# Gate and value products of a convolution and SwiGLU kernel: from f32 products in a 15-product form to three float32r passes in an 11-product form

## The chip, the cores and the metric

The kernel runs on one core of a Trainium2 chip. Its engines are TensorE (PE, with its weight loads shown apart as PEld), VectorE (DVE), ScalarE (ACT), GpSimd (POOL) and SyncE (SP), which issues most DMA transfers. Work is kept in SBUF, matmuls write to PSUM. The metric is the device time of one execution in microseconds (us); the kernel before takes 2593.32 us, the median of three runs (2593.27 to 2593.45).

## The reference

Eight sequences of 4096 tokens of width 192 pass a causal convolution of seven taps, the same taps for the 24 channels of a head, and the result passes a gated feed-forward block without bias:

```python
w = np.exp(weight - max); w = w / (sum(w) + 1e-09)          # 8 heads x 7 taps
out[b, s, h] = sum_k w[h, k] * x_pad[b, s + k, h]           # x: (8, 4096, 192)
x = out.reshape(32768, 192)
xn = x / sqrt(mean(x * x) + 1e-06) * rms_g
g = xn @ w_gate;  val = xn @ w_val                          # (192, 1536) each
return (g / (1 + exp(-g)) * val) @ w_out                    # (1536, 192)
```

All arrays are f32 or are read as f32.

## The kernel before, in words

**Tiling.** Tokens are taken in 32 *pairs* of 2 x 512. Width 192 is three slices of 64 rows. Gate weights lie on partitions 0 to 63 and value weights on 64 to 127, and so does x, twice; so each product is two half instructions (64 rows by 128 columns of weights, 512 tokens), one for the gate and one for the value, on the two halves of the array at once. The 1536 hidden channels are 12 blocks of 128.

**Products.** Pair 0 is computed plainly (`plain`, L1052, and `outer`, L1093) while the weights, which come as 64-bit floats, are being converted. From pair 1 on, four *units* of three channel blocks each need 18 products (three slices, two token groups, three blocks); the table `CHAINS` of the class `Unit` reaches them with 15 products (L794) on sums of weights (`WSUM`, made once on POOL, L365/L369) and sums of x (`XSUM`, L705, on DVE and POOL for each pair). Products run into each other in PSUM: copies of a bank (L743 on ACT, L747 on DVE) fork a chain, sums (L810, L814, L820, L826) join it, silu (L839) and a product (L846) make the hidden activations `ht`.

**Output.** A seven-product form of the output matmul takes sums of `ht` (L962, POOL) and 42 *steps*, each of six column-tiled matmuls (L934); its results are joined (L983), transposed (L949) and stored (L1016).

**What a pair prepares for later pairs.** `load_heads` brings x (L146); the taps (`part_tap`, L468 on ACT, then L476 on DVE) accumulate in PSUM; squares (L492), a reduction (L503), a power (L512) and a scaling (L530) give the normalized x, which is stored to a scratch tensor in DRAM (L670) and fetched back, transposed, as `xb` (L696).

**Order.** The order is written out by hand and by tables: `ORDER` is one string of words, run once for each pair. `p2` emits two steps of TensorE; other words name an engine (A, V, G, D) and an action. Every engine runs its instructions in the order in which they were emitted, and waits on semaphores for others.

The printed functions below are those that the change touches.

Of the kernel before, what the change touches and what calls it, by code (L numbers as in the profile page):

```python
# [11 lines left out]
F32 = mybir.dt.float32  # L12
AF = mybir.ActivationFunctionType
ALU = mybir.AluOpType
# [5 lines left out]
def kernel(  # L20
# [45 lines left out]
    XOP = (5, 6, 9, 0, 15, 14, 4, 7, 13, 10, 2, 11, 12, 8, 3)  # L66
    XSUM = (
        (0, 1, 4), (1, 2, 6), (2, 0, 6), (9, 3, 5), (3, 3, 8), (4, 7, 15), (5, 4, 15), (6, 5, 7),
        (7, 0, 1), (8, 1, 2), (9, 8, 15),
    )  # L70
    WSUM = (
        (9, "sub", 5, 2), (9, "sub", 9, 8), (10, "sub", 1, 4), (10, "add", 7, 10),
        (11, "sub", 1, 8), (7, "sub", 7, 11), (11, "sub", 4, 11), (12, "add", 1, 6),
        (4, "sub", 12, 4), (5, "sub", 5, 4), (5, "add", 3, 5), (13, "sub", 2, 6),
        (13, "add", 0, 13), (14, "sub", 3, 12), (3, "sub", 6, 3), (0, "add", 0, 3),
        (3, "sub", 3, 2), (6, "neg", 6, 6), (8, "neg", 8, 8),
    )
    WAT = (7, 9, 2, 0, 1, 4, 5, 11, 14, 6, 10, 12, 8, 3, 13)

    SPAN = 1509
    ORDER = (  # L90
        "p2 GX4- VT11- p2 AS40.0.0 GX9- AS40.1.0 p2 AF0.1.0 AF0.0.0 p2 VC.0.0 Dload- p2",
        "VC.1.0 AS41.0.0 VS41.1.0 p2 AS00.1.0 VS00.0.0 p2 Vbc- VD5.0.0 Gmul- p2 VD5.1.0",
        "AS42.0.0 VS42.1.0 AS51.1.0 p2 AS51.0.0 VR1.0.0 p2 VR1.1.0 VR0.0.0 p2 AF2.0.0 VN.1.0",
        "AG0.0.0 p2 VR0.1.0 AF3.0.0 Dplace- AF3.1.0 p2 GM0.1.0 VR2.0.0 p2 VR2.1.0 AS44.1.0",
        "AS44.0.0 VR5.1.0 p2 AG2.0.0 VR3.0.0 p2 GM2.1.0 AS40.0.1 VR3.1.0 AS40.1.1 p2 VR5.0.0",
        "AG4.0.0 p2 VM4.1.0 AF0.0.1 AG5.0.0 VF0.1.1 p2 AG1.0.0 VS41.0.1 GM5.1.0 p1 AS41.1.1",
        "p1 VC.0.1 AG3.0.0 p1 VC.1.1 p1 GM3.1.0 VS00.0.1 p2 AS42.0.1 VS42.1.1 AS00.1.1 GS3.0",
        "p2 VD5.0.1 p1 VD5.1.1 p1 AS51.0.1 GS1.0 VR1.0.1 AS51.1.1 p2 VR1.1.1 AF2.0.1 GS3.1 p2",
        "AF2.1.1 VR0.0.1 AG1.0.1 p1 VR0.1.1 p1 GM1.1.1 VF3.0.1 AF3.1.1 p2 AG0.0.1 VR2.0.1 p1",
        "VR2.1.1 p1 GM0.1.1 AS44.0.1 AS44.1.1 VR5.0.1 p2 GS2.0 VR5.1.1 p2 AS40.0.2 VR3.1.1",  # L100
        "AS40.1.2 p1 VR3.0.1 GM1.1.0 p1 AG4.0.1 AG3.0.1 p1 VM4.1.1 p1 GM3.1.1 VF0.0.2 AF0.1.2",
        "p2 AS41.0.2 VS41.1.2 p1 AG5.0.1 p1 VC.0.2 GM5.1.1 p1 VC.1.2 p1 AS00.0.2 AS00.1.2 p2",
        "GS1.1 AS42.1.2 AS42.0.2 p2 VD5.0.2 GS3.2 p1 VD5.1.2 p1 AS51.0.2 VR1.0.2 AS51.1.2 p2",
        "GS2.1 VR1.1.2 AF2.0.2 p2 AF2.1.2 VR0.0.2 GS1.2 AG1.0.2 p1 VR0.1.2 p1 AG0.0.2 VF3.0.2",
        "GM1.1.2 p1 AF3.1.2 p1 VR2.0.2 AG2.0.1 p1 VR2.1.2 p1 AS44.0.2 GM2.1.1 AS44.1.2 p2",
        "VR3.0.2 AG2.0.2 GS2.2 p1 VR3.1.2 p1 AS40.0.3 VR5.0.2 AS40.1.3 p2 GM2.1.2 AG4.0.2",
        "VR5.1.2 AG3.0.2 p1 VM4.1.2 p1 AF0.0.3 GM0.1.2 p2 AF0.1.3 VS41.0.3 AS41.1.3 p2",
        "GM3.1.2 AG5.0.2 VC.0.3 p1 VC.1.3 p1 AS00.1.3 GS3.3 AS00.0.3 p2 VS42.0.3 AS42.1.3 p2",
        "GS1.3 VD5.0.3 p1 VD5.1.3 p1 AS51.0.3 GM5.1.2 VR1.0.3 AS51.1.3 p2 VR1.1.3 AF2.0.3 p2",
        "GS2.3 AF2.1.3 VR0.0.3 AG1.0.3 p1 VR0.1.3 p1 GS4.2 VF3.0.3 AF3.1.3 p2 AS44.0.3",  # L110
        "VS44.1.3 p1 GM1.1.3 p1 VR5.1.3 p1 VR5.0.3 p1 Acv0_1 VR3.0.3 AG5.0.3 p1 Vcv1_1 Acv0_2",
        "GM5.1.3 p2 VR3.1.3 AG0.0.3 p2 AG3.0.3 Vcv1_2 DfetA GS3.4 p1 AG4.0.3 p1 VR2.0.3 p2",
        "Acv0_0 Vcv2_2 GM3.1.3 p2 VM4.1.3 p2 Vcv2_1 Ac1 GS3.5 p1 AG2.0.3 p1 Vcv3_1 p2 GS1.4",
        "Vcv3_2 p2 Vcv1_0 p2 GS2.4 p1 Vcv2_0 p2 Vcv4_1 p1 As7 GS1.5 DfetB Dst0- p1 VR2.1.3 p2",
        "Vcv5_1 p1 GM0.1.3 p1 Vcv3_0 p2 Vcv6_1 p1 GS2.5 p1 Vcv4_0 p2 Vcv4_2 GS4.0 p2 Vcv5_0",
        "p2 GS4.1 p1 Vcv6_0 p2 Vcv5_2 Ac2 p1 GX0 p1 Vcv6_2 p2 VM2.1.3 Asq p2 GS4.4 p4 VX3 p1",
        "GS4.3 p4 VX6 p1 GX2 p2 VC22 p2 VX1 p2 GS4.5 VT22 p2 Vred p2 GX8 p3 GX7 p2 VC21 p2",
        "VT21 Gpow p2 VX5 p2 VX10 p2 VT12 p1 Dst1 p1",
# [16 lines left out]
    def load_heads(p, b, t0):  # L135
# [4 lines left out]

        def get(dst, tb, h, dims, r):
            row = x[b, t0 + tb * TB + r - HALO, h * GS :]
            src = bass.AP(
                tensor=row.tensor, offset=row.offset, ap=[dims, [D, TB + HALO - r], [1, GS]]
            )
            nc.sync.dma_start(out=dst, in_=src)  # L146

        first = 0
        if t0 == 0:
            nc.gpsimd.memset(t[0:H, 0:HALO, :], 0.0)  # L150
            get(t[0:H, HALO:, :], 0, 0, [GS, H], HALO)
            first = 1
        for h in range(H):
            get(t[first * H + h :: H], first, h, [TB * D, P // H - first], 0)
# [206 lines left out]
    def w_sums(u):  # L361
        t = wf[u]
        for i, (d, op, a, b) in enumerate(WSUM):
# [9 lines left out]
            if i % 4 == 3:  # L373
                yield
# [935 lines left out]
```

## Time and profile before

| what | value |
|---|---|
| median of 3 runs | 2593.32 us |
| span of the profiled execution | 2591.8 us |
| TensorE busy, granted clock | 2580.5 us, 1.00 |
| DVE, POOL, ACT busy | 2298.8, 2190.6, 1553.5 us |
| first product of pair 1 | at 126.37 us |
| products of one pair, then output steps | 51.92 us, 27.44 us |
| a stretch 1000 to 1052 us (products): DVE, ACT, POOL busy | 45.75, 42.31, 41.37 us |
| a stretch 1052 to 1079.4 us (output): DVE, ACT, POOL busy | 25.76, 5.78, 27.09 us |
| DMA | 137.33 MB, 53 GB/s on the mean |

The profile is one execution. In a group's row stand the line, the engine and operation, the tiles out and in with their shapes, the count, the busy time and mean duration of one, and the idle time ahead of it with its releaser. Matmuls are pipelined, so the mean of one is longer than the distance between two. The chain of work that ended last names at each step what released it; shares of it, not of busy time, tell what sets the end.

### The profile page before, as it was taken

Reading aid. Unit: us, or ns where it says so; the run is one execution under the profiler, and the core shown is the slowest. Engines: PE = TensorE matmul, PEld = TensorE weight load, DVE = VectorE, ACT = ScalarE, POOL = GpSimd, SP = SyncE. Lnnn points to the kernel's source line nnn. Section 1 sums busy time; section 2 is a strip of 40 time slices with the busy share of each in tenths; the row PEclk is TensorE's granted clock in tenths of the full one; section 3 lists DMA queues with packets and bytes.
Section 4 is the critical chain, followed back from the end, with each engine's and each line's share of the span. In section 5 each row is a group of like instructions: output and inputs, shape, how many; then the busy total and the mean of one; then the engine's idle time right before and its main releaser. Section 6 shows DMA issues by size and latency. Waiting matters only on the chain.

```text
span 2591.8 us, 60798 instructions
## 1 busy us (share of the span) xinstructions
PE 2580.5 (100%) x23872; PEld 1778.0 (69%) x23872; DVE 2298.8 (89%) x3681; ACT 1553.5 (60%) x2825; POOL 2190.6 (85%) x1791
## 2 busy tenths in 40 slices
PE   9999999999999999999999999999999999999999
PEld 6876666767667666676666676666766666766667
DVE  8898898988989989989889899899898898988975
ACT  6576555675555765556755557655566555676554
POOL 4898888988889888898888898888988888988877
PEclk9999999999999999999999999999999999999999
DMA  6232332222331323322223313233222233122210
GB/s 145 57 57 33 63 64 52 44 45 51 63 63 38 57 33 64 63 49 47 45 51 64 62 38 55 36 63 63 46 49 45 52 63 58 37 56 40 50 44 14
DMA packets 512397, 137.33 MB, mean 53 GB/s; under 512 B 483950, under 2 KB 486510, under 8 KB 512110
## 3 DMA queue, kind: packets, MB, share of 16 engines
q1 hardware_dynamic: 508364, 132.53, 27.2%
q8 instruction: 187, 3.06, 0.5%
q10 hardware_dynamic: 3746, 0.92, 0.2%
q14 instruction: 100, 0.82, 0.1%
HBM read 83.84 MB, written 49.55 MB: 51 GB/s over the span
## 4 chain that ended last, share of the span: by engine, by line
PE 99%; DVE 0%; issue 0%; DVEq 0%
PE ps L794 62%; PE ps L934 33%; PE ps L1052 2%; PE ps L1093 1%; DVE xb L647 0%; DVE wf L338 0%; DVE xc L333 0%; DVE o_sb L949 0%; DVE xc L298 0%; DVE xc L303 0%; DVE xc L306 0%; DVEq L1305 0%
## 5 line engine op out<-in xcount | busy, mean ns | idle before, releaser
L794 PE MATMUL ps<-xc,wf 64*128 64x512 f32 x4960 | 1214.0, 591 | 0.0
L794 PEld LDWEIGHTS ps<-xc,wf 64*128 64x128 f32 x4960 | 681.3, 186 | 375.3 <-issue 176.7
L794 PE MATMUL ps<-xb,wf 64*128 64x512 f32 x2480 | 679.7, 591 | 0.0
L743 ACT ACTIVATE tile<-ps 128x512 f32<-128x512 f32 x678 | 391.1, 593 | 389.0 <-PE ps L794 295.3
L743 ACT ACTIVATE tls<-ps 128x512 f32<-128x512 f32 (+1 forms) x562 | 323.5, 589 | 438.6 <-PE ps L794 222.0
L846 POOL TENSOR_TENSOR ht<-ht,tile 128x512 f32<-128x512 f32 x329 | 418.9, 1275 | 141.0 <-ACT tile L839 65.2
L794 PEld LDWEIGHTS ps<-xb,wf 64*128 64x128 f32 x2480 | 353.9, 187 | 182.9 <-issue 93.6
L846 POOL TENSOR_TENSOR ht<-ht,tls 128x512 f32<-128x512 f32 x260 | 330.6, 1274 | 86.4 <-ACT tls L839 38.8
L743 ACT ACTIVATE ps<-ps 128x512 f32<-128x512 f32 (+1 forms) x589 | 336.0, 580 | 87.9 <-PE ps L934 32.6
L962 POOL TENSOR_TENSOR early<-ht 128x512 f32<-128x512 f32 x279 | 354.8, 1276 | 4.9
L476 DVE SCALAR_TENSOR_TENSOR ps<-xh,tp,ps 128x512 f32<-128x512 f32 x450 | 320.3, 748 | 4.0 <-ACT ps L468 1.8
L934 PE MATMUL ps<-ht,wo_sb 128*32 128x128 f32 (+2 forms) x5208 | 318.5, 380 | 0.0
L934 PEld LDWEIGHTS ps<-ht,wo_sb 128*32 128x32 f32 x5208 | 233.9, 110 | 81.7 <-POOL ht L846 23.5
L934 PE MATMUL ps<-ht,x 128*32 128x128 f32 (+2 forms) x4464 | 250.7, 379 | 0.0
L826 DVE TENSOR_TENSOR tile<-ps,tile 128x512 f32<-128x512 f32 x349 | 237.4, 683 | 10.2 <-PE ps L794 5.0
L962 POOL TENSOR_TENSOR ht<-ht 128x512 f32<-128x512 f32 x186 | 239.0, 1285 | 4.9
L826 DVE TENSOR_TENSOR ht<-ps,tile 128x512 f32<-128x512 f32 x328 | 222.5, 680 | 6.5 <-ACT tile L743 6.5
L934 PEld LDWEIGHTS ps<-ht,x 128*32 128x32 f32 x4464 | 184.3, 110 | 61.3
L839 ACT ACTIVATE tile<-tile 128x512 f32<-128x512 f32 x349 | 214.5, 625 | 0.0
L826 DVE TENSOR_TENSOR ht<-ps,tls 128x512 f32<-128x512 f32 x292 | 199.0, 681 | 6.8 <-ACT tls L743 3.6
L826 DVE TENSOR_TENSOR tls<-ps,tls 128x512 f32<-128x512 f32 x271 | 184.9, 683 | 17.0 <-PE ps L794 13.8
L934 PE MATMUL ps<-early,x 128*32 128x256 f32 (+2 forms) x3348 | 196.0, 379 | 0.0
(149 smaller groups left out, 3278.1 us busy)
## 6 DMA issues: line engine op xcount, KB each, us to landing
xb<-xd SPq DMA_DIRECT2D x120, 384.0 KB
xd<-yn SPq DMA_DIRECT2D x244, 96.0 KB
xh<-in_x_dram SPq DMA_DIRECT2D x192, 105.0 KB
out_dram<-o_sb SPq DMA_DIRECT2D x122, 96.0 KB
out_dram<-o_sb SPq DMA_DIRECT2D x60, 128.0 KB
xh<-in_x_dram SPq DMA_DIRECT2D x56, 98.4 KB
out_dram<-o_sb SPq DMA_DIRECT2D x122, 32.0 KB
ht<-in_moe_w_gate_dram SPq DMA_DIRECT2D x12, 192.0 KB
```

The source lines that it names most:

```text
L476: nc.vector.scalar_tensor_tensor(out=dst, in0=xk, scalar=w, in1=at, op0=ALU.mult, op1=ALU.add)
L743: nc.scalar.activation(out=dst, in_=src, func=AF.Copy, scale=float(s))
L794: nc.tensor.matmul(out=self.new(v, h, True) if first else self.old(v, h), lhsT=wf[self.u][HALF[h], WAT[i], :], rhs=x_op(XOP[i])[HALF[h]], ...
L826: nc.vector.tensor_tensor(out=self.hv(v) if h else t[:], in0=self.old(v, h), in1=t[:], op=plus(s))
L839: nc.scalar.activation(out=t[:], in_=src[:], func=AF.Silu)
L846: engine[eng].tensor_tensor(out=self.hv(v), in0=src, in1=t[:], op=ALU.mult)
L934: nc.tensor.matmul(out=self.bank(b)[i * Q : (i + 1) * Q, at : at + n], lhsT=left, rhs=cols, start=fresh, stop=True, skip_group_check=True, ...
L962: engine[eng].tensor_tensor(out=dst, in0=a, in1=b, op=op)
L1052: nc.tensor.matmul(out=bank(h, bks[h])[:], lhsT=wf[u][HALF[h], AT[h][k] * NF + f, :], rhs=xb[HALF[h], g, k, :], start=(k == 0), stop=(k == ...
L1093: nc.tensor.matmul(out=bank(h, bks[h])[:, w : w + D], lhsT=hts[f // NF][HALF[h], g, f % NF, j * P : (j + 1) * P], rhs=wo_sb[HALF[h], f, :] ...
```

## The change

The gate and value products of pairs 2 to 31 are done in float32r. Each operand is split: `high` is the number with its low 12 bits masked off (`HIGH`), the rest is the low part. Of each weight piece and of each x operand three parts are kept, and three passes, accumulated in PSUM, give the product: high by high, a scaled low part of the weight by the low part of x, and a third pass with parts chosen so that the scaled sums add up; a common factor is taken into the normalization (`factor`).

The form changes too. Instead of four units with 15 products there are six blocks `j` of two channel blocks, each with 11 products (P1 to P7 and Q1 to Q4) for 12 plain ones. They accumulate in four *duos* of PSUM banks, gate and value side by side, named a, b, c, d after the four results of a block. P1 and Q1 go into a; a is copied to b (`f1`, ACT, 1024 columns); P5 and Q2 go into c, copied to a buffer (`f3`, ACT); after P6 into b, `f4` (DVE) writes b plus buffer to c, after P7 `f5` (DVE) writes b plus buffer to d; P2, P3, P4 and Q3, Q4 complete them. `g` is the silu, `m` the product with the value, `h1` to `h4` the sums for the output form, `o1` to `o7` its steps.

x: `x_sum` makes five sums on POOL, and `split` makes the parts of five operands: `k` (mask, DVE), `n` (copy, ACT), `l` (plain difference, DVE), `d` (scaled difference, DVE). They are written in the buffers that the products read, once these are done with them.

Weights: nine combinations of each block are prepared once during pair 1 (`prepare`), split into three parts and stored to DRAM (`wd`); from there each pair loads 54 pieces of 128 x 384 words into a ring of 12 slots (`ring_load`, on SP, when the slot's last product has been emitted). Pair 1 computes its products plainly in f32 (L907).

The taps go back to whole tiles of 1536 columns in SBUF (`tap`, L437; the first on ACT), stores to scratch, fetches and head loads are spread over the order. The new `ORDER` places a few output steps of the pair before (`p1-`) among the products of the next; `LINE` gives the order of TensorE, `FIRST` the order of pair 1. A trailing + or - names a later or an earlier pair. Lines below are those of the diff; L936 of the changed kernel is its product, L961 its output step.

```diff
+    LINE = (
+        "P1.0 Q1.0 P5.0 Q2.0 P6.0 P2.0 Q3.0 P7.0 P3.0 P4.0 Q4.0 P1.1 Q1.1 P5.1 Q2.1 P6.1 P3.1",
...
+        "P7.4 P3.4 P1.5 P4.4 Q4.4 Q1.5 P5.5 Q2.5 P6.5 P2.5 o1.0 o1.2 o1.1 o1.3 o1.4 o7.0 P7.5",
+        "Q3.5 P3.5 o7.1 o1.5 Q4.5 P4.5 o7.3 o7.4 o6.0 o6.4 o2.3 o2.4 o6.1 o7.2 o6.2 o7.5 o2.1",
...
+    ORDER = (
+        "VT21- p2 Af1.0 p3 Af3.0 Spl.0+ Gh4.0- p1- Vf4.0 p1 Acv0++ p2 Aga.0 p1 p1- Spl.1+",
...
+        "Gx2+ p1 Gx4+ p1 Gh1.4 Vk.3+ p1 Vd.3+ p1 Gh2.0 Vf4.5 An.3+ p1 Gh3.3 p2 Vl.3+ Aga.5 p1",
+        "Vk.0+ p1 Gh3.4 Vma.5 Asq++ Agc.5 Gh2.1 Vf5.5 p1 Vd.0+ Vmc.5 An.0+ p1 Agd.5 Sld.2+++",
...
+    NSLOT = 12
...
+    def ring_load(slot):
+        n = next(taken)
+        q, (j, o) = 2 + n // len(pieces_of), pieces_of[n % len(pieces_of)]
+        if q >= PAIRS:
+            return
...
+        nc.sync.dma_start(out=ring[0][:, slot, :], in_=wd[r : r + P, :])
...
+    def split(act, g, eng):
+        src = operand(g)
...
+        high = tt[:, 4 : 4 + n, :]
+        if act == "k":
+            nc.vector.tensor_scalar(
+                out=high.bitcast(U32), in0=src.bitcast(U32), scalar1=HIGH, scalar2=None,
+                op0=ALU.bitwise_and,
+            )
+            return
+        if act == "n":
+            copy(eng, split_of(g, 0).bitcast(F32R), high)
+        elif act == "l":
+            e.tensor_tensor(out=split_of(g, 1).bitcast(F32R), in0=src, in1=high, op=ALU.subtract)
+        else:
+            nc.vector.scalar_tensor_tensor(
+                out=split_of(g, 2).bitcast(F32R), in0=high, scalar=1.0 + SPLIT, in1=src,
+                op0=ALU.mult, op1=ALU.subtract,
+            )
...
-            nc.tensor.matmul(
-                out=self.new(v, h, True) if first else self.old(v, h),
-                lhsT=wf[self.u][HALF[h], WAT[i], :], rhs=x_op(XOP[i])[HALF[h]],
-                start=first, stop=True, skip_group_check=True,
-            )
...
+            for q in range(3):
+                left = ring[0][:, slot, q * P : (q + 1) * P].bitcast(F32R)
+                right = split_of(g, q)[:, i, :].bitcast(F32R)
                 for h in range(2):
+                    nc.tensor.matmul(
+                        out=self.both(j, c)[:, h, :], lhsT=left[HALF[h]], rhs=right[HALF[h]],
+                        start=(first and q == 0), stop=True, skip_group_check=True,
+                    )
+            left_of[key] -= 1
+            if left_of[key] == 0:
+                ring_load(slot)
...
+            if act == "f1":
+                self.open((j, "b"), True)
+                copy(eng, self.both(j, "b"), self.both(j, "a"))
+            elif act == "f3":
+                copy(eng, s5, self.both(j, "c"))
+            elif act in ("f4", "f5"):
+                c = "c" if act == "f4" else "d"
+                if c == "d":
+                    self.open((j, c), True)
+                nc.vector.tensor_tensor(
+                    out=self.both(j, c), in0=self.both(j, "b"), in1=s5, op=ALU.add
+                )
```

## The prediction

> **What bounds the kernel now.** I read the page's busy shares, then the chain that ended last in order of time, then the groups of each engine with their shapes kept apart, then a stretch of the timeline.
>
> ```profile
> PE 2580.5 (100%) x23872; PEld 1778.0 (69%) x23872; DVE 2298.8 (89%) x3681; ACT 1553.5 (60%) x2825; POOL 2190.6 (85%) x1791
> 32.40 62.17 PE ps L1052 x271
> ...
> 94.58 31.31 PE ps L1093 x380
> ...
> 126.37 51.72 PE ps L794 x239
> ...
> 1051.18 27.44 PE ps L934 x337
> 1078.62 51.92 PE ps L794 x240
> ```
>
> TensorE is never idle: from 126.37 us a pair takes 51.92 of gate and value products (L794) and 27.44 of output steps (L934), 79.36 in all. 126.37 + 31 x 79.36 = 2586.5, and the tail to the span's end, 2591.8, is 5.3. About 1.5 lies around the span (median 2593.3). Runs agree within 0.2 us, so 0.2% (5 us) is what can be told from no change.
>
> ```profile
> L794 PE MATMUL ps<-xc,wf 64*128 64x512 f32 x4960 | 1214.0, 591 | 0.0
> L794 PEld LDWEIGHTS ps<-xc,wf 64*128 64x128 f32 x4960 | 681.3, 186 | 375.3 <-issue 176.7
> L826 DVE TENSOR_TENSOR ht<-ps,tile 128x512 f32<-128x512 f32 x328 | 222.5, 680 | 6.5 <-ACT tile L743 6.5
> L810 DVE TENSOR_TENSOR ps<-ps,tile 128x512 f32<-128x512 f32 x156 | 104.8, 694 | 28.9 <-PE ps L794 24.0 <-ACT tls L743 4.5
> L705 DVE TENSOR_TENSOR xc<-xc 128x512 f32<-128x512 f32 x62 | 43.9, 707 | 3.2
> L452 DVE SCALAR_TENSOR_TENSOR y<-xh,tp,y 128x1536 f32<-128x1536 f32 x6 | 11.6, 1935 | 0.0
> ```
>
> A pair has 60 f32 products, each in two half arrays side by side; every instruction shows as two records, so 240 records in 51.92 us: 865 ns a product. A weight load of 186 ns hides behind each record.
>
> ```profile
> 1066.01 1.10 DVE L846 TENSOR_TENSOR ht<-ht,tls 128x512 f32<-128x512 f32 x1
> 1067.04 1.77 DVE L705 TENSOR_TENSOR xc<-xb 128x512 f32<-128x512 f32 x1
> ...
> 1066.51 1.74 POOL L962 TENSOR_TENSOR tls<-ht,nt 128x512 f32<-128x512 f32 x1
> 1068.21 1.73 POOL L962 TENSOR_TENSOR more<-ht,nt 128x512 f32<-128x512 f32 x1
> ```
>
> This is the second thing to see. A DVE sum with both inputs in SBUF, 0.7 us elsewhere, took 1.10 and 1.77 here, and POOL's 1.28 became 1.74: they take turns. POOL, begun at 66.51, ends 1.28 after DVE's end at about 67.0; DVE, begun at 67.04, ends 0.7 after that.
>
> **Products.** Per pair from the second on, 60 f32 products go and 66 x 3 = 198 float32r passes come (the changed program's order has 396 half instructions a pair). No row shows such a pass. An f32 product is two records of 432 ns; from above a pass costs a whole record. From below: an f32 product must combine two halves of each operand, four partial products in 865 ns, so one costs 216. A pass is one such product of 12-bit parts; I take 216 and keep 433 as a rival. 198 x 0.2163 = 42.8 us. The output steps stay 42 of the same shapes: 27.44. TensorE's floor is 70.27 a pair, 9.1 less. (The Trainium skill, FP8 and Floating Point Precision, "TensorE Precision Notes": true FP32 is four passes; it gives no time for float32r.) The issue rate is one the trace has: 396 instructions in 42.8 us are 108 ns each, the 252 of the output steps in 27.44 are 109.
>
> **Pair 1 and the ends.** Pair 1 is done plain in f32: 144 half instructions, as many as L1052's, 62.2, with the output steps 89.6. Pair 0 keeps its 126.4; the weight sums leave POOL, which was not on the path. The nine weight pieces are prepared beside pair 1's products: per piece two DVE, two ACT, one or two POOL instructions of 768 columns and a store; by the rows 1.7 us of DVE each, 15 in all, in 62 us that else hold 24 multiplies (16.3) and six taps (11.6): nothing. But the splits for pair 2 overwrite the buffers of the plain weights and pieces, and its x lands where plain products read, so fetch (about 8 us, as the two fetches of one pair here), two or three POOL sums (3) and the DVE splits, multiplies and reduction before Q1 (about 17, with turns 21) run after the last plain product: 32 us against 36 output steps (23.5) and P1: 8 us once, 0 to 15.
>
> **DVE, per later pair** (72 instructions counted in the order, 113 before): 24 multiplies of 0.680, 16.3; 12 sums from PSUM of 1024 columns (694 at 512, and 1.04 ns a column between 384 and 512: 1.23), 14.7; six taps over 1536, now SBUF to SBUF, of 1.94, 11.6; five splits: the mask 0.82 (a bitwise row, 384 in 425 ns, 1152 in 895) or 0.50, 3.8; the scaled difference at L452's rate 5.8; the plain difference (0.707 + 0.53) 5.7; transposes 2.9, output sums 1.1, reduction 2.4. 64.3, and as neighbours overlap by some 60 ns, 60: it fits into 70.3.
> **ACT**: 24 silus, 12 copies of 1024 (1.03), the splits' copies, the rest: 36. The copies a->b and c->buffer stand two products (1.30) before their reader: hidden; an ACT 0.3 late would show on TensorE. **POOL**: 24 + 5 sums of 1.28, scaling 2.9, power 2.6: 43, where 68 were.
>
> **Turns at the port.** The taps and the splits' differences are two-input SBUF instructions of DVE, beside POOL's sums. Most falls into the output stretch: ten differences (11.5) there against some 14 POOL sums and the power and scaling. A DVE instruction that finds POOL running waits between 0 and 1.28; I take 0.62. Where it decides: after the last P6 DVE has mask, difference, f4, difference, mask, multiply, f5 in its queue, 7.3 us less overlaps, and Q4 of the last block, due 7.2 after P2, waits for f5. Three or four waits, 2.2, come on top of about 6: some 1.1 late. Behind f5 the remaining splits queue, and P1 and Q1 of the next pair wait for those; there the 41 steps (26.7) cover 21 of DVE work and 6 of turns. Another 1.0 I put to the product stretch: DVE 38.9 with six taps that wait, in 43.4. Bounds 0 and 13.5 (all 15 instructions of the five splits a whole turn of 1.28, less the 5.7 of slack there): 2.1, near the low end, as the trace's own output stretch has turns and no stall.
> The Trainium skill, SBUF - State Buffer, "Who interferes with whom", says that a single-source operation in two-port mode takes the pair as well. By that the five masks would wait too, 5 x 0.62 = 3.1 more, and the total would be 2496; no row here shows a mask beside POOL.
>
> **DMA and SP.** New: 54 ring loads of 197 KB a pair, 10.6 MB. Before, DMA share 0.27 of 79.4: 21.4 us. The nearest rows: 128-partition loads of 1536-byte rows moved 371 GB/s (44 to 46 us), the 64-partition fetch 211 at share 1.04.
>
> ```profile
> 44.00:46.00 2.00, 1.00 1.06 371
> 1054.00:1056.00 2.00, 1.00 1.04 211
> ```
>
> 29 to 52 us, so 50 to 74 of 72; the first row has the same shape, so it hides. A load waits for its slot's last product; behind it on SP stand the later loads, the stores to scratch, fetches, head loads and output. One load is used per 0.79 us; 12 slots are 9.5 us ahead, against an issue of 0.6 to 0.74 (80 issues, 48 to 59 us) and a few us to land. If that lead is gone, TensorE waits at once.
>
> **Sum.** 126.4 + 89.6 + 8 + 30 x (70.27 + 2.1 = 72.4) + 5.3 + 1.5 = 2403. Break-even: (2593.3 - 230.8) / 30 = 78.75 a pair.
>
> **Rivals.**
> 1. All covered: 70.3 to 71 a pair, no hand-over, 2331 to 2361. For it: now DVE is busy 25.76 of 27.40 in an output stretch with such turns, and TensorE does not wait. 0.14.
> 2. DMA as the new bound: at the fetch's rate 42 loads in the product stretch (39) with 13 of scratch and fetch are 52 against 46.7, 5 late: 77.5 a pair, 2556; or turns of 4 to 8, 74.5 to 78.7: 2466 to 2592. Together 0.16.
> 3. Slower by the port: if turns cost 8.5 or more a pair, it passes break-even; all whole turns give 83.8, 2745. Port demand in the output stretch is 23 of POOL and 11.5 of DVE against 26.7, which speaks for it; that a third of POOL's may slide speaks against. 0.09.
> 4. Slower by the pass: at 433 ns products take 85.7, a pair 115, 3680. Decides from 248 ns a pass. 0.08.
> 5. The weight load is not covered: a half array would wait for its own load, 216 + 186 = 402 ns, 79.6 a pair's products, 109, 3504. That loads hid under records twice as long leaves it open. The Trainium skill, TensorE: Matmul & The Clock Gate, "The mechanism" of Part 3, says that a weight load overlaps running matmuls only for another row group; by it f32 records would now be 433 + 186 apart, and they are 433, so the trace differs. 0.05.
>
> That it does not do what it says is excluded: 11880 float32r half instructions stand in the order.
>
> **How the numbers follow.** The forecast, 71 to 74.5 a pair, has 0.46. Faster 0.46 + 0.14 + 0.16 = 0.76, same 0.02, slower 0.22. From the floor 2331, set at 2335, to 2625 (79.8 a pair, a third of rival 3) about 0.8 is held; the far cases 4 and 5 stay outside.
>
> **What would show it.** L936 records 216 ns apart in a stretch of about 43 to 46 us with L961 steps between; the chain in pieces of about 72 a pair; waits of PE on DVE's f5 near 1 us a pair; DVE's split differences at 1.2 to 2.5; the ring as no releaser. Records 400 ns apart would make it wrong at once; PE waiting on DMA ring or on the splits by over 8 us a pair would turn the sign.

## The result and the profile after

The changed kernel takes 2843.8 us (2839.7 to 2849.3), against 2593.3 before: 1.097 times as long, 95% interval 1.095 to 1.098. The forecast was 2403, with a range up to 2625. The profiled execution took 2841.6 with a span of 2839.7.

First the page's busy shares, then one window with the busy time of each engine (columns: window, length, busy us and instructions of PE, PEld, DVE, ACT and POOL, granted clock, DMA share, GB/s). The window is about one pair from the steady part.

```profile
PE 2588.1 (91%) x28600; PEld 1871.5 (66%) x28600; DVE 2190.1 (77%) x2357; ACT 1138.0 (40%) x1559; POOL 1678.7 (59%) x1110
```

```profile
1000.00:1085.00 85.00, 78.69 (x902) 57.89 (x901) 68.83 (x71) 34.77 (x46) 52.99 (x35) 1.00 0.66 171
```

TensorE, without a gap before, is now idle 6 us of a pair of 85, and no other engine is full: DVE 69, POOL 53, DMA 0.66. So there is no single bound to read off the shares. The groups say where TensorE waits (columns: instructions by line, engine, operation and tile; busy us, mean ns; idle time before them and what ended it):

```profile
L936 PE MATMUL ps<-part,ring 64*128 64x512 f32 x11880 | 1517.6, 400 | 90.5 <-ACT ps L698 35.9 <-DMA ring<-wd 29.1 <-DVE ps L1005 16.9
L936 PEld LDWEIGHTS ps<-part,ring 64*128 64x128 f32 x11880 | 1104.4, 185 | 462.0 <-ACT ps L698 91.2 <-DVE ps L1005 65.2 <-issue 52.2
L1005 DVE TENSOR_TENSOR ps<-ps,tt 128x1024 f32<-128x1024 f32 x360 | 443.5, 1232 | 216.8 <-PE ps L936 113.4 <-ACT tt L698 96.5 <-DVE ht L1018 0.5
L961 PE MATMUL ps<-ht,x 128*32 128x384 f32 x2232 | 407.9, 490 | 85.7 <-ACT ps L698 59.7 <-ACT tt L698 17.7 <-POOL ht L988 8.3
L835 DVE TENSOR_SCALAR tt<-xb 128x1024 uint32<-128x1024 uint32 x90 | 118.5, 1317 | 6.4
L835 DVE TENSOR_SCALAR tt<-tt 128x512 uint32<-128x512 uint32 x30 | 87.4, 2913 | 33.0 <-ACT part L698 32.7 <-DVE s L508 0.3
```

The releasers of TensorE are the copies f1 and c1 (L698 into PSUM), the ring loads and the sums f4 and f5 (L1005); the sums wait in their turn for products (113.4) and for the copy f3 (L698 into `tt`, 96.5). The prediction had f1, f3 and the ring down as hidden, f5 as late in the last block alone, and did not price c1. Of the 59.7 of L961, 27.2 belong to the start (below). The durations that were estimated from neighbouring rows are right (f4 and f5 1.23 us as forecast), except where an instruction met POOL's work: the masks of L835 above all, at 1317 and 2913 ns for a forecast of 820 and 500.

The mean of 400 ns is a modelled one. The distance from one start to the next is more telling. Worked out from the starts in the trace over the middle of the run, ten pairs of each kernel, in us per pair (the ten of the changed kernel add up to 85.2 a pair):

```
                              before    after
pass to pass                   51.41    51.29     (before: 60 f32 products, after: 198 float32r passes)
last pass to first step         0.52     3.10     (before once a pair, after six times)
step to step                   27.21    29.57
last step to first pass         0.20     1.22
```

198 passes at 216 ns would be 42.8 us in place of 54.4 (the first two rows). Of the distances between passes of the same ten pairs, 1606 are under 245 ns (median of all 231), 217 lie at 290 to 370, 47 at 370 to 460 and 40 above 700.

The start comes late as well. The timeline around the hand-over from the plain to the split form (columns: start, length, engine, line, operation; in brackets the idle time before and what ended it; SPq is SP's DMA queue):

```profile
204.81 2.85 PE L907 MATMUL ps<-xb,part 64*128 64x512 f32 x12 [0.34 <-DVE ht L1018]
210.74 3.46 PE L961 MATMUL ps<-ht,wo_sb 128*32 128x384 f32 x60
...
214.67 7.90 SPq L804 DMA_DIRECT2D ring<-wd  x12
...
223.61 4.20 SPq L662 DMA_DIRECT2D xb<-xd  x6
...
234.71 1.26 POOL L862 TENSOR_TENSOR tt<-xb 128x512 f32<-128x512 f32 x1 [21.66 <-DMA xh<-in_x_dram]
...
240.55 1.04 ACT L698 CAST part<-tt 128x1024 fp32r<-128x1024 f32 x1 [27.04 <-DVE tt L835]
243.99 2.79 PE L961 MATMUL ps<-ht,x 128*32 128x384 f32 x24 [27.20 <-ACT ps L698]
...
255.05 1.51 PE L961 MATMUL ps<-ht,x 128*32 128x384 f32 x12 [8.27 <-POOL ht L988]
...
274.47 1.43 PE L936 MATMUL ps<-part,ring 64*128 64x512 f32 x10
```

The first split product starts at 274.5 where the forecast's terms put it at 224. TensorE waits 27 us for c1, and c1 does not need the new x at all: it is queued on ACT behind the split copy (CAST), which waits for DVE's mask, for POOL's x sum, and for a fetch that SP issues behind twelve ring loads. (The profile names the head load xh as what released POOL; L862 reads xb, so what it needs is the fetch, next to that load in the queue.)

So the profiled 2841.6 = 274.5 to the first split product + 30 x 84.9 + 18.2 that are left over at both ends of these + 1.9 around the span, where the forecast had 224 + 30 x 72.4 + 5.3 + 1.5. The 12.5 us a pair are 375 of the 441.

### The profile page after: what moved, and what is told of

The parts are those of the page before. It is cut to its first block, busy times and chain, and to the rows that moved or that the text cites. A ratio compares the mean times of both kernels' runs of the same rounds, so it can differ in the third digit from the quotient of the medians.

```text
span 2839.7 us, 69721 instructions
## 1 busy us (share of the span) xinstructions
PE 2588.1 (91%) x28600; PEld 1871.5 (66%) x28600; DVE 2190.1 (77%) x2357; ACT 1138.0 (40%) x1559; POOL 1678.7 (59%) x1110
## 5 line engine op out<-in xcount | busy, mean ns | idle before, releaser
L936 PE MATMUL ps<-part,ring 64*128 64x512 f32 x11880 | 1517.6, 400 | 90.5 <-ACT ps L698 35.9
L936 PEld LDWEIGHTS ps<-part,ring 64*128 64x128 f32 x11880 | 1104.4, 185 | 462.0 <-ACT ps L698 91.2
L1011 ACT ACTIVATE tt<-ps 128x512 f32<-128x512 f32 x744 | 443.7, 597 | 825.1 <-PE ps L936 763.2
L1018 DVE TENSOR_TENSOR ht<-ps,tt 128x512 f32<-128x512 f32 x744 | 510.8, 688 | 255.0 <-ACT tt L1011 240.7
L1005 DVE TENSOR_TENSOR ps<-ps,tt 128x1024 f32<-128x1024 f32 x360 | 443.5, 1232 | 216.8 <-PE ps L936 113.4
L988 POOL TENSOR_TENSOR ht<-ht 128x512 f32<-128x512 f32 x372 | 587.2, 1598 | 24.1 <-PE ps L961 19.3
L961 PE MATMUL ps<-ht,x 128*32 128x384 f32 (+2 forms) x6696 | 417.2, 382 | 85.7 <-ACT ps L698 59.7
L961 PE MATMUL ps<-ht,wo_sb 128*32 128x384 f32 (+2 forms) x6696 | 423.9, 383 | 0.8 <-DVE tt L1035 0.8
L961 PEld LDWEIGHTS ps<-ht,x 128*32 128x32 f32 x6696 | 286.9, 110 | 195.9 <-POOL ht L988 81.7
L961 PEld LDWEIGHTS ps<-ht,wo_sb 128*32 128x32 f32 x6696 | 290.6, 110 | 124.4 <-issue 36.3
L698 ACT COPY tt<-ps 128x384 f32<-128x384 f32 (+1 forms) x242 | 213.0, 880 | 362.2 <-PE ps L961 331.4
L437 DVE SCALAR_TENSOR_TENSOR y<-xh,tp,y 128x1536 f32<-128x1536 f32 x180 | 344.8, 1916 | 0.0
L988 POOL TENSOR_TENSOR ht<-hs,ht 128x512 f32<-128x512 f32 x186 | 296.0, 1612 | 51.8 <-PE ps L961 49.5
L698 ACT COPY ps<-ps 128x1024 f32<-128x1024 f32 (+1 forms) x211 | 194.5, 922 | 250.0 <-PE ps L936 194.8
L698 ACT CAST part<-tt 128x1024 fp32r<-128x1024 f32 (+1 forms) x150 | 144.1, 960 | 136.8 <-DVE tt L835 136.8
L835 DVE TENSOR_SCALAR tt<-tt 128x1024 uint32<-128x1024 uint32 (+1 forms) x60 | 140.9, 2348 | 61.5 <-ACT part L698 32.7
L961 PE MATMUL ps<-hs,x 128*32 128x128 f32 (+2 forms) x2232 | 139.6, 381 | 46.2 <-DVE tt L1035 46.2
L961 PEld LDWEIGHTS ps<-hs,x 128*32 128x32 f32 x2232 | 97.8, 110 | 80.8 <-DVE tt L1035 54.5
L862 POOL TENSOR_TENSOR tt<-xb 128x512 f32<-128x512 f32 x30 | 50.5, 1683 | 140.4 <-DMA xb<-xd 78.4
```

What stands on the lines that cost most here:

```text
L437: nc.vector.scalar_tensor_tensor(out=y, in0=xk, scalar=w, in1=y, op0=ALU.mult, op1=ALU.add)
L698: nc.scalar.copy(out=dst, in_=src)
L835: nc.vector.tensor_scalar(out=high.bitcast(U32), in0=src.bitcast(U32), scalar1=HIGH, scalar2=None, op0=ALU.bitwise_and,)
L862: engine[eng].tensor_tensor(out=dst, in0=a, in1=b, op=op)
L936: nc.tensor.matmul(out=self.both(j, c)[:, h, :], lhsT=left[HALF[h]], rhs=right[HALF[h]], start=(first and q == 0), stop=True, skip_group_c ...
L961: nc.tensor.matmul(out=self.acc(b)[i * Q : (i + 1) * Q, at : at + n], lhsT=left, rhs=cols, start=fresh, stop=True, skip_group_check=True, ...
```

## The experiments

The length of a pair is, from here on, the median distance between the starts of one DVE reduction (L488 in the changed kernel) that comes once a pair. By it: before 79.4, after 84.8. The four runs that are given without an interval below (one_pass, one_pass_no_h, lean_no_chain, lean_no_silu) are single executions.

**The price of a pass.** The question behind two rivals is settled by rows of matmuls with nothing beside them.

```
for i in range(96): for h in range(2):   # L56 f32, L63 float32r; L70 full rows; L77 one half; L98 bf16
    nc.tensor.matmul(out=ps[..], lhsT=w[HALF[h]], rhs=x[HALF[h]], ...)
```

> Leaves the whole computation out: eight rows of 96 products each on data of x, to price a pass by itself. In the changed kernel a float32r pass of two half arrays takes about 252 ns, where 216 was forecast. Theory L, the weight load is not fully covered: halves with 64 weight columns come near 216, halves with 256 tokens stay well above 126. Theory I, a fixed time for each instruction (126 ns for a half): full rows, one instruction a pass, take 216; halves take 252 with 512 and with 256 tokens alike, and with 64 weight columns. Theory S, the stream itself is slower for float32r: 252 in halves and in full rows, 126 with 256 tokens. f32 halves should show 433 a record in each, bf16 halves 216 in theory S and L.

The timeline of that run, TensorE alone:

```profile
8.47 84.10 PE L56 MATMUL ps<-mov,sta 64*128 64x512 f32 x384 [8.47 <-ACT sta L35]
92.00 22.37 PE L63 MATMUL ps<-mov,sta 64*128 64x512 f32 x192
114.31 22.08 PE L70 MATMUL ps<-mov,sta 128*128 128x512 f32 x96
136.31 21.62 PE L77 MATMUL ps<-mov,sta 64*128 64x512 f32 x94
...
191.81 20.90 PE L98 MATMUL ps<-mov,sta 64*128 64x512 bf16 x191
```

Start to start, once the row runs evenly, an f32 product of two halves takes 0.858 (the first two are slower, so the whole row of 96 takes 84.1), a float32r pass 0.227, in halves, full rows or one half alone, and a bf16 pass 0.216. So a pass costs 5% more than the forecast's 216 ns, not 433 and not 402. In the row with one half the next load, 184 ns, goes into the same rows that are being multiplied, and is covered all the same. The Trainium skill's rule (TensorE: Matmul & The Clock Gate, "The mechanism" of Part 3: loads overlap for another row group only) would give about 0.41 there.

**Semaphores and turns.** The 217 distances near 335 ns had two explanations: a wait that is passed but costs, or a real stop.

```
+ first pass of each product reads a weight tile that DVE wrote long before      (rates_waits)
+ 16 turns of 6 passes and 3 output steps, against one block of each             (rates_turns)
+ each sixth pass waits for an ACT copy of the bank before                       (rates_turns)
```

> Four rows of 96 passes over 512 columns in half arrays, by themselves; the reference is not computed. First f32, then float32r into adjacent banks with every pass closed as in the changed kernel, then the same with the first pass of each product of three reading a weight tile that DVE wrote long before (a semaphore already passed), then f32 with the same. Theory W: a pass of the changed kernel is 0.227 to 0.231 us, and a pass that carries a wait starts its weight load only after the pass before, whether the wait is long satisfied or not, and costs some 0.105 more (distances of 335 ns stand 217 times in ten pairs of the changed kernel's trace). Then the rows take 84, 21.8, 21.8 + 32 x 0.105 = 25.2, and for f32, whose halves run 433 ns a record, 84 to 87. Rival E: the 335 ns are semaphores that really come 0.1 late; then the third row takes 21.8 like the second. Rival C: the layout (adjacent banks, every pass closed) makes the pass itself longer; then the second row takes 24.

The four rows took 84.5, 22.2, 21.8 and 82.0 us (the first two with a slow start, the last to the start of its last record); the distance between passes is 227 ns in the second row and in the third: a semaphore already passed costs nothing, nor do adjacent banks. Theory W fell, E holds: the 335 ns are real stops.

> Rows by themselves; the reference is not computed. 96 float32r passes in half arrays and 48 output steps of six column tiles in one block each, then the same in 16 turns of six passes and three steps; then 48 f32 products and 48 steps in the same two ways; then rows in which each sixth pass (float32r, then f32) waits for an ACT copy of the bank before it, so that the semaphore is really late. Theory S (a stop of the pass stream, by a late semaphore or by steps in between, costs an uncovered weight load on the next pass but one: 0.203 then 0.333 after steps, 341 then 338 ns after a late wait, 315 instead of 227 into the steps): 21.8 and 31.4 in blocks, 53.2 + 15 x 0.3 = 57.5 in turns; after the wait the second distance is 0.335 for float32r. For f32 with records of 433 ns the same stop is covered: turns within 2 us of blocks (42 + 31.4), and the second distance 0.43. Rival: the stop costs the same in both forms (the load after a stop is never covered).

In one block 48 steps took 31.3, 0.653 each, and 96 passes 24.2, the first of them 421 ns apart as TensorE starts; with the 0.227 of the row before, one turn of six passes and three steps should take 6 x 0.227 + 3 x 0.653 = 3.32, and it took 3.67. A turn costs 0.35. The distances show where: 313 to 315 ns out of the passes, 203 back in, and 333 to 338 for the second pass. After a late semaphore the distance from the waiting pass to the next is 336 to 337: a stopped TensorE pays 0.106 once it goes on. That a weight load then lies open is what the load records suggest (they start with their own matmul there); it was not tried apart. For f32 the same: 3 products and 3 steps took 4.86 against 3 x 0.863 + 1.96 = 4.55, the second distance 527 in place of 422. The rival (equal cost in both forms) holds. The kernel before had one such turn a pair and never stopped; the changed one has six turns and some twenty stops.

**One load at a time.** Four runs leave out one thing each.

```
fixed_ring:  +if n < NSLOT:  nc.sync.dma_start(out=ring[0][:, slot, :], ...)      # no reload
no_h_sums:   +if p == 1:     self.h_sum(...)
no_splits:   +if p == 2:     split(act, i, eng)
no_chain:    +if p == 2:     f1, f3 (copies) and f4, f5 (sums)
```

> Leaves out all ring loads but the first twelve, so later products use wrong weights; all else stays. If the new DMA traffic holds TensorE (rival 2 of the prediction), a pair gets 4 or more us shorter: 2720 or less. If the ring is covered and only its few late loads show (29 us of waits in all), 2800 to 2835.

> Leaves out POOL's sums of the hidden activations for the output form from pair 2 on, so that DVE finds POOL's port free nearly always. If turns at the port cost 2 us a pair, as forecast, 2780; if 8, 2600. If the stalls come from chains of PE, ACT and DVE alone, within 20 us of 2844.

> Leaves out the four splitting instructions of each of five operands (15 on DVE, 5 on ACT) from pair 3 on, so products use old parts of x. If the splits decide when the next pair's first products start, or hold f4 and f5 of the last block, 3 to 6 us a pair go: 2660 to 2750. If only the pass price and the chains inside a block matter, 2810 or more.

> From the second of the split pairs on, the copies f1 and f3 and the sums f4 and f5 between the products of a block are left out (part of the computation is missing), so no product waits for a PSUM copy or sum of its own block; products, splits, ring, silus and multiplies stay. Theory W+Q (the pair of 85.2 is 198 passes at 0.231, some 27 loads uncovered behind waits at 0.105 to 0.2, and late DVE and ACT work in the product stretch): some 15 uncovered loads (1.8) and the gaps at f1, f3, f4, f5 (about 3) go, and DVE has 14.7 less: 4 to 7 us a pair, 2640 to 2725. Rival C (a longer pass from sharing the chip with the other engines): only the gaps go, 2 to 3 us a pair, 2755 to 2785.

```
               us       ratio to before (95%)      a pair
after        2843.8     1.097 (1.095 to 1.098)      84.8
fixed_ring   2816.3     1.086 (1.083 to 1.089)      84.1
no_h_sums    2796.6     1.078 (1.075 to 1.082)      83.2
no_splits    2811.6     1.084 (1.081 to 1.087)      83.5
no_chain     2777.1     1.071 (1.068 to 1.075)      82.1
```

Each is worth 0.7 to 2.7 us a pair, and none alone is the cause. fixed_ring and no_splits came in where a covered ring (2800 to 2835) and splits that do not decide (2810 or more) were expected, no_h_sums between its expectations. no_chain missed theory W+Q (2640 to 2725) and lies in the range of rival C (2755 to 2785), a longer pass; the next runs decide on C. no_h_sums shows the turns at the port well: without POOL's sums of the hidden activations a mask takes 0.69 to 0.73 us, and yet the pair gains only 1.6. Its groups:

```profile
L835 DVE TENSOR_SCALAR tt<-xb 128x1024 uint32<-128x1024 uint32 x90 | 64.3, 714 | 8.6 <-ACT part L698 2.3
L835 DVE TENSOR_SCALAR tt<-tt 128x512 uint32<-128x512 uint32 x30 | 21.8, 728 | 79.3 <-ACT part L698 79.0 <-DVE s L508 0.3
```

1317 became 714 ns and 2913 became 728: a pair's masks take 8.6 us beside POOL's sums and 3.6 without. In the changed kernel one of them stood a whole POOL instruction through:

```profile
1297.98 2.96 POOL L516 TENSOR_TENSOR yn<-y,s 128x1536 f32<-128x1536 f32 x1
...
1298.16 3.06 DVE L835 TENSOR_SCALAR tt<-tt 128x512 uint32<-128x512 uint32 x1 [1.10 <-ACT part L698]
```

**TensorE by itself.** All four left out together, and then the silus and multiplies as well.

```
bare:        fixed_ring + no_h_sums + no_splits + no_chain
bare_alone:  bare, +if p <= 2: silu (L1011), multiply (L1018)
bare_blocks: bare, ORDER "VT21- p6- p2 Af1.0 ..." in place of five "p1-"/"p2-" between the products
```

> Ring reloads, h sums, splits and the copies and sums between products all left out from the second or third split pair on (part of the computation is missing); 198 passes, 252 output instructions, silus, multiplies, taps and the reduction stay. Theory W+Q: what is left is 198 x 0.231 + 27.4 = 73.2 a pair and up to 1.5 of waits for silus and multiplies; with the start as it is (first split product at 274): 2475 to 2520. So faster than the kernel before by 3 to 4 per cent, and less than the 2403 forecast by the start and the pass price alone. Rival C: passes stay at 0.252 with everything else gone: 77.3 a pair, 2600.

> As bare, and the silus and multiplies are left out too from the second split pair on, so that no product waits for a bank (still more of the computation is missing). Theory S: 198 x 0.227 = 44.95, steps 27.4, six islands 1.7, and under 1 of waits in the output stretch: 74.3 to 75.2 a pair, 2530 to 2560; TensorE's own floor is 4 to 5 a pair above the 70.27 forecast. Rival C: 77, as bare, passes and steps are longer for another reason.

> As bare, but the six output steps that a pair leaves to the next stand in one block ahead of its products, not in three islands between them (the same parts of the computation are missing). Theory S: an island costs 0.088 on the way in, 0.1 on the way out and 0.106 on the second pass, 0.29 together; three fewer are 0.9 a pair: 77.15 becomes 76.2, 2618.7 becomes 2590 to 2595. Rival: the turns are covered by other waits; the pair stays within 0.3 of 77.15.

bare took 2618.7 (1.009, 1.007 to 1.011), 77.15 a pair; bare_alone 2591.8 (0.9995, 0.9985 to 1.0004), 76.3 a pair:

```profile
1300.00:1376.30 76.30, 74.95 (x902) 57.72 (x900) 18.49 (x21) 4.39 (x5) 15.06 (x11) 1.00 0.29 54
```

With next to nothing left but TensorE's own work the changed kernel only draws level with the one before. A pair of bare_alone, in the rows of the table above: 44.43, 1.89, 28.80, 1.21. That is 198 x 0.227 = 44.95 of passes, 27.4 of steps, five turns more than before (1.8), and 2.0 for two waits in the output stretch, for the copies and sums of the output (L698, L1035 of the changed kernel), which now stand only one or two steps ahead of their readers. It missed its expected 74.3 to 75.2, mainly by these two waits, of which under 1 was expected. By their times bare (2475 to 2520 expected by theory W+Q, 2600 by C) and bare_alone (77 by C) speak rather for C. The passes themselves do not: of 1919 distances between passes in ten pairs of bare_alone, 1859 are under 245 ns, with a median of 227, so passes of 0.252 are excluded and the rest is turns and waits.

bare_blocks missed: 2626.6 (1.013, 1.011 to 1.014) and 77.55 a pair, no gain. Three turns less are in the trace, but the six steps in front now wait for DVE, as the islands had not (bare's waits first, then those of bare_blocks; columns: total us, times, longest):

```profile
PE ps L962 <- DVE tt L1040: 24.2, 32, 0.8
```

```profile
PE ps L962 <- DVE tt L1040: 45.1, 62, 0.8
```

**The start.** In the order for pair 1, the ring's first loads go behind the fetch, and the x sums and first splits behind the work of pair 1.

```
-"... Sld.0+++ R p1 Agb.5 ..."  "... Sft.1+ Gx1+ Gx3+ Gx5+ Gx2+ Gx4+ Vk.3+ Vd.3+" "An.3+ Agd.5 p1 Vmd.5 ..."
+"... Sld.0+++ p1 Agb.5 ..."    "... Sft.1+ R Agd.5 p1 Vmd.5 ... Ac1 Gh2.5 Gx1+ Gx3+ ... Vk.3+ Vd.3+ An.3+ ..."
```

> Everything is computed. In the order of the first split pair's eve, the twelve first ring loads go behind the fetch of x, and the x sums and first splits go behind the last silus, multiplies and h sums of pair 1 and behind c1. Theory H (the 27 us stall at c1 and the 8 us at an h sum are ACT and POOL instructions queued behind splits and sums that wait for the fetch, which SP issues behind twelve ring loads): c1 comes at its time, and the first split product comes at 240 to 255 instead of 274: 2809 to 2825. Rival M: x itself is late, whatever is queued: the wait moves from c1 to the first split product, and the time stays within 8 us of 2843. In both the steady pair stays at 85.2.

It took 2828.3 (1.0895, 1.0873 to 1.0918), 15 less and just above theory H's 2809 to 2825; the first split product starts at 255.6, 19 earlier, and the pair stays at 84.8. The 27 us at c1 are gone, but a 12.6 us stall at the next such copy came:

```profile
218.14 1.51 PE L961 MATMUL ps<-ht,x 128*32 128x384 f32 x24 [0.66 <-ACT ps L698]
223.16 0.86 PE L961 MATMUL ps<-ht,x 128*32 128x384 f32 x12 [3.52 <-POOL ht L988]
...
241.13 5.56 PE L961 MATMUL ps<-ht,x 128*32 128x384 f32 x60 [12.55 <-ACT tt L698]
```

Theory H holds for c1; the rest is the length of fetch, sums and splits itself, M's share.

**The rest without TensorE.** If TensorE alone took 76.3, what made 84.8? Two runs take passes away.

```
-for q in range(3):
+for q in range(2):      # two_pass; range(1): one_pass; one_pass_no_h: also no_h_sums
```

> Only the first of the three passes of each split product is made (the products are not exact then); all the rest stays. It shows what the other engines and their chains allow if TensorE were nearly free: 132 passes less are 30 us a pair. Theory S (DVE, busy 68.8 of 85.2 with its waits, is close behind TensorE, and its order is as tight): the pair falls only to 70 to 78, 2360 to 2600, with TensorE waiting on DVE and ACT most of what was won. Rival T (TensorE and its passes alone set the pair): 55 to 60, 1940 to 2090.

> Two of the three passes of each split product are made (the products are not exact then); all the rest stays: TensorE has 66 passes, 15 us a pair, less to do. Theory L (what bounds the pair is the loop of TensorE, ACT's copies and silus and DVE's sums and multiplies through DVE's one queue, some 82 us a pair with its splits and taps in between; TensorE, 76.3 alone, runs inside that loop): the pair falls from 84.9 only to 82 to 84, 2750 to 2815. Rival T (TensorE's own time sets the pair, and the 82 of the one-pass form is its lower granted clock of 0.79): the pair falls by most of the 15, to 70 to 74, 2390 to 2510.

> One pass, and POOL's h sums left out from the second split pair on (part of the computation is missing). Theory L: POOL's sums cost the loop the turns at the port alone, 1.4 to 3 a pair: 2655 to 2705. Rival P (POOL, busy 52 of 82 with long waits, is itself the loop): the pair falls by over 8, below 2500.

two_pass took 2770.0 (1.069, 1.067 to 1.071), 83.0 a pair; one_pass 2745.8, 81.9; one_pass_no_h 2672.6, 78.9. By the price of a pass, 15 us of TensorE less gain 1.8 and 30 gain 2.9. Both theories of one_pass missed (70 to 78, and 55 to 60); one_pass_no_h came in as theory L expected (2655 to 2705), and not as the rival that has POOL as the loop (below 2500). A window of about a pair of each:

```profile
1000.00:1083.00 83.00, 67.34 (x780) 46.69 (x770) 68.53 (x73) 34.05 (x46) 53.29 (x35) 0.96 0.68 178
```

```profile
1000.00:1082.00 82.00, 61.87 (x644) 38.97 (x640) 68.48 (x72) 33.94 (x46) 51.96 (x35) 0.79 0.69 180
```

Theory L is borne out by two_pass: with TensorE busy 67 of 83 us the engines with their waits on each other still take 83 a pair, each with time to spare (DVE 68.5 busy). one_pass adds less than it seems to. From 1040 to 1060 us, a stretch of products, its granted clock was 0.50, and over ten pairs its passes stand 0.427 apart (median), so a product of one pass took about what one of two passes, 0.235 apart, takes in two_pass. The little that one_pass gains beyond two_pass therefore doesn't show what TensorE's products at full clock would leave.

**DVE's load or the round trips.** One pass, with the splits' two differences left out (12 bits of each factor are multiplied, another precision), a third of the ring's bytes, and the start of hand_over; then the same with a piece of the block's round taken out.

```
lean:           range(1); split: only the mask and its copy; ring_load [:, slot, 0:P]; FIRST of hand_over
lean_no_chain:  lean, +if p == 2: f1, f3, f4, f5
lean_no_silu:   lean, +if p <= 2: silu, multiply
```

> Only the high parts are multiplied (12 bits of each factor, so it isn't the precision of the change): one pass, the mask and the copy of each split stay, the two differences of each split are left out, the ring loads a third of the bytes, and the hand-over is that of the run before. DVE has some 14 us a pair less, TensorE 30. Theory L (the loop is paced by what DVE has in its queue): 82 - 14 = 66 to 70 a pair, less about 15 at the start: 2240 to 2380. Rival R (the round trip PE, ACT, DVE of each block sets the pair, however full DVE is): 77 or more, 2560 or more.

> As lean, and the copies f1 and f3 and the sums f4 and f5 are left out from the second split pair on (part of the computation is missing). Theory R (a block of the six runs through one round trip over the four bank pairs: the bank freed by a multiply, f1, products, f4, products, f5, products, silu, multiply, 8.2 us in lean, six times 49): without f1, f4 and f5 the round is some 4.5 shorter, 27 a pair: 50 to 60 a pair, 1750 to 2080. Rival Q (DVE and POOL with their taps, sums and port turns set the pair): DVE loses 14.7, the pair falls to 66 to 72, 2220 to 2420.

> As lean, and the silus and multiplies are left out from the second split pair on (part of the computation is missing). Theory R: the round of a block loses two silus, two multiplies and their hand-overs, about 3.5 of 8.2: 21 a pair, 55 to 62, 1900 to 2130. Rival Q: DVE loses 16.3, ACT 14: the pair falls to 64 to 72.

lean took 2607.8 (1.006, 1.004 to 1.007), 78.4 a pair: against one_pass, DVE has 15 us less (53.5 busy), the pair only 3.5.

```profile
1000.00:1078.40 78.40, 61.73 (x638) 38.43 (x638) 53.50 (x62) 33.91 (x46) 45.90 (x35) 0.76 0.46 98
```

Theory L for this run, the pair paced by DVE's load, missed with its 66 to 70; R's 77 or more held. That speaks for the round trips (R). The timeline of lean shows one such round, from one f1 to the next:

```profile
1299.27 2.26 DVE L437 SCALAR_TENSOR_TENSOR y<-xh,tp,y 128x1536 f32<-128x1536 f32 x1
1299.44 1.00 ACT L698 COPY ps<-ps 128x1024 f32<-128x1024 f32 x1 [0.81 <-DVE ht L1013]
1300.35 1.02 ACT L698 COPY tt<-ps 128x1024 f32<-128x1024 f32 x1
1300.49 1.65 PE L931 MATMUL ps<-part,ring 64*128 64x512 f32 x6 [1.26 <-ACT ps L698]
1301.45 1.22 DVE L1000 TENSOR_TENSOR ps<-ps,tt 128x1024 f32<-128x1024 f32 x1
...
1302.58 1.27 DVE L1013 TENSOR_TENSOR ht<-ps,tt 128x512 f32<-128x512 f32 x2
1302.72 2.07 PE L931 MATMUL ps<-part,ring 64*128 64x512 f32 x8 [0.58 <-DVE ps L1000]
1303.98 1.23 DVE L1000 TENSOR_TENSOR ps<-ps,tt 128x1024 f32<-128x1024 f32 x1
...
1305.36 2.08 PE L931 MATMUL ps<-part,ring 64*128 64x512 f32 x8 [0.57 <-DVE ps L1000]
1306.24 0.60 ACT L1006 ACTIVATE tt<-ps 128x512 f32<-128x512 f32 x1 [1.24 <-PE ps L931]
1306.87 0.69 DVE L1013 TENSOR_TENSOR ht<-ps,tt 128x512 f32<-128x512 f32 x1 [1.07 <-ACT tt L1006]
...
1307.65 1.00 ACT L698 COPY ps<-ps 128x1024 f32<-128x1024 f32 x1 [0.81 <-DVE ht L1013]
```

The steps follow each other closely: f1, products, f4, products, f5, products, silu, multiply, and the multiply frees the bank pair into which the next block's f1 copies. 8.2 us, six times a pair. Two places are not the round's alone. f4 (1301.45) starts only as the tap before it on DVE (L437, to 1301.53) and f3 (to 1301.37) end, and f5 (1303.98) comes right behind two multiplies (to 1303.85); so DVE's queue is a part of this round. And its products ran at a granted clock of 0.50 (1299.44 to 1307.65), 0.43 to 0.59 us apart; at full clock the round would be shorter, by how much no run shows.

Without f1, f3, f4 and f5 lean falls only to 70.1 a pair (2367.8), without silus and multiplies to 71.6 (2409.7), not to the 50 to 62 that R alone would give, but to what rival Q gave (66 to 72, 64 to 72). A part of both gains may be the clock, since it rose from 0.79 to 0.90 and 0.86 in these runs. Other waits come up at once, such as that for the ring in lean_no_chain:

```profile
1337.94 3.29 PE L931 MATMUL ps<-part,ring 64*128 64x512 f32 x14 [4.57 <-DMA ring<-wd]
```

So the round is one of several lengths that lie close together; R and Q both hold in part, and how much of the 82 each owns is left open.

## Why the prediction was wrong

The direction was wrong, and the step that failed is TensorE's floor being taken as the pair: "TensorE's floor is 70.27 a pair" plus 2.1. In its place the runs show two lengths above it: TensorE's own work takes 76.3 as it is ordered here (bare_alone), and the engines with their waits on each other hold the pair at 83.0 even with a third of the passes left out (two_pass). In the order in which things were left out, the 12.4 us between 72.4 and 84.8 are, within 0.1:

```
pass of 227 ns in place of 216 (rates), 198 x                       2.1
five more turns between passes and steps at 0.35 (rates_turns)       1.8
two waits in the output stretch that stay in bare_alone              2.0
silus and multiplies (bare less bare_alone)                          0.8
ring, h sums, splits, f copies and sums (after less bare)            7.7
less the 2.1 that the forecast had for turns at the port            -2.1
```

In another order the shares would differ: the four things of the fifth row are worth 6.3 when left out one at a time, and 7.7 together.

- **"I take 216 and keep 433 as a rival"**: right in kind, 5% off; 2.1 a pair.
- **The output steps "stay 42 of the same shapes: 27.44"**: their number stayed, their place did not. Mixing them with the products cost 1.8, and output copies close to their readers 2.0. The order was at hand; turns were costed at nothing without a word, and that is a missing term.
- **"It fits into 70.3"** of DVE: this is the main error, not in the number but in what was concluded from it. DVE's busy time was nearly right (68.8 with its turns, 60 + turns forecast). But DVE works in order and waits, for silus 240.7 us and for products 113.4 in the whole run, so busy time that fits into the pair does not mean that the queue does. With a third of the passes gone the pair stays at 83.0, and with 15 us less of DVE's own work it falls by 3.5 (one_pass to lean).
- **"The copies a->b and c->buffer stand two products before their reader: hidden; an ACT 0.3 late would show on TensorE"**: the second half came true. Two products were 1.30 us; f1 needs a bank, which a multiply has to free (52.2 us of ACT's waits, L698 on L1018), then 1.0 for itself. The waits of these two lines (columns: total us, times, longest):

```profile
DVE ht L1018 <- ACT tt L1011: 240.7, 260, 7.9
ACT ps L698 <- DVE ht L1018: 52.2, 65, 1.1
```

- **Turns at the port, 2.1, bounds 0 to 13.5**: taking POOL's sums out is worth 1.6 a pair (3.0 with one pass, 81.9 to 78.9), which is the size of the forecast, though these runs also spare the steps their waits for the sums; the place was not well judged. The masks' turns were set at nothing, and the masks lost 5.1 of DVE's time a pair. The Trainium skill (SBUF - State Buffer, "Who interferes with whom"), by which a single-source operation in two-port mode takes the shared pair too, is borne out by 1317 against 714 ns; the 2496 that the forecast gave by it is still 348 short.
- **DMA and SP, "it hides"**: nearly: 0.7 a pair.
- **Hand-over 8, 0 to 15**: 36, the second term that was mis-sized (63.7 from the last plain product to the first split one, with 27.4 of steps in it). It counted the DVE and POOL work, but not what is queued behind it: c1 on ACT and h sums on POOL; nor the twelve ring loads ahead of the fetch on SP. The plain products took 76.0 in place of 62.2, waiting for multiplies queued behind the weight pieces ("nothing" in the forecast), and pair 0 took 8.3 more, which no run looked into.
- **Rivals**: 4 and 5 (a pass at 433 or 402) are excluded. 2 and 3 each named something that exists, at 0.7 and 1.6 a pair, far below what they needed. Two of their sums were off: 71 a pair without a hand-over is 2353, not 2361 (rival 1), and turns of 4 to 8 are 74.3 to 78.3 a pair, 2459 to 2579 (rival 2); neither changes a conclusion. What came true in part, a round trip through all engines that is longer than any engine's busy time, was not among them. It could have been read from the order: at the forecast's own durations f1, f4, f5, one silu and one multiply are 4.8 of a block (1.03 + 1.23 + 1.23 + 0.60 + 0.68, the silu by the profile after), and the products that stand between them in that chain come on top, against 7.1 for all eleven products of the block.

The break-even of 78.75 assumed a start of 224. With the start at 274.5 it is (2591.4 - 274.5 - 18.2) / 30 = 76.6, which only bare_alone reaches, and it draws.

## What to carry to other kernels

A busy share says what an engine must do, not how long its queue takes: before a floor is cut, follow one block through all engines (who frees the bank, who copies, who waits) and add the durations along that loop. When an engine that never waited is made faster, count the stops: here each one on TensorE cost its own length and 0.1 us more, and each change from products to column-tiled steps and back 0.35. And of work moved to a turning point between two forms, look at what stands behind it in every queue, since the stall shows at an instruction that needs none of it.

## What was not expected of the hardware

- A float32r pass over 512 columns takes 227 ns alone, 5% above bf16 (216) and 0.26 of an f32 product (858).
- A semaphore already passed costs TensorE nothing (227 ns a pass with 32 of them in 96 passes, and without); a stop costs some 105 ns beyond its own length, in float32r (333 for 227) and f32 (527 for 422).
- The granted clock went down where TensorE had less to do: 1.00 with 198 passes in 85 us, 0.96 with 132 in 83, 0.79 with 66 in 82, but 0.90 with 66 in 70 (lean_no_chain, over two pairs). In lean's round above it was 0.50, though TensorE was busy 5.8 of its 8.2 us and never idle for more than 1.3. By what rule, no run shows; passes left out are in part paid back in slower ones.
